# Quarter chunks in the softmax's gaps, two value chunks in one PSUM tile, and weights loaded before the last segments

## The chip, the cores and the metric

The kernel runs on one core of one Trainium2 chip. The metric is the device time of that core in microseconds (us). A kernel is timed in several executions, beside the kernel before on the same chip. In the lines of the profile PE is TensorE (PEld its weight loads), DVE is VectorE, ACT is ScalarE, POOL is GpSimd, and SPq is the DMA queue that the SP engine issues to.

## The reference, cut to what matters

Two blocks, each run twice: attention with a recurrent memory, then a gated feed-forward block.

```python
for s in range(n_seg):                      # 64 segments of 32 tokens
    h = concatenate([mem, xs])              # 8 memory rows + 32 tokens, 512 wide
    q, k, v = h @ Wq, h @ Wk, h @ Wv        # 32 heads of 128
    p = softmax(where(mask, q @ k.T * scale, -1e9))
    o = (p @ v) @ Wo
    mem = o[:8]                             # the next segment needs this
...
z = gelu(x @ w_in); z1 = z[..., :Fh]; z2 = layernorm(z[..., Fh:])
out = (z1 * (w_sp @ z2 + b_sp)) @ w_out     # Fh = 688
...
x = x + attn(ln(x)); x = x + ff(ln(x)); x = x + attn(ln(x)); x = x + ff(ln(x))
```

The 64 segments depend on one another through `mem`, so a microsecond on the path of one segment counts 128 times. The kernel reads only eight tokens of each segment later (the "last tokens" of the change); their work is cut into chunks that TensorE runs as fills while a segment waits.

## The kernel before

Three PSUM tags hold the attention's accumulators; PSUM is the memory that TensorE writes, and it is divided into banks. A tag with two buffers (`acc`) serves many tiles in turn; `attO` is one buffer of four banks.

```python
pers = ctx.enter_context(tc.tile_pool(name="a_pers", bufs=1))     # oB, VB, KTB, QTB of the last tokens
...
acc = _Tagged(ps_pool, "acc", 2)
att = _Tagged(ps_pool, "att", 1)
attO = _Tagged(ps_pool, "attO", 1)
...
# one segment, from the first scores on
scores(0)                                    # TensorE, then exp on ScalarE
qk_T(3, r3)
v0 = attO.tile([P, 4, 512], F32, name="psv0")
v_mm(0, v0[:, 0, :])                         # first value chunk, 16 matmuls
close(0)                                     # mask, VectorE
v_out(0, v0[:, 0, :])                        # cast, VectorE
scores(1)
close(1)
v1 = acc.tile([P, 512], F32, name="psv1")    # second chunk: another tile
v_mm(1, v1[:])
v_out(1, v1[:])
psM = acc.tile([P, 512], F32, name="psM")    # sums for the memory rows
...
psO = attO.tile([P, 4, 512], F32, name="psO")
pv(0)
...                                          # psD: sums for the tokens
pv(1)
...                                          # 1/x as exp(-ln x) of psM (Rm) and psD (Rt), ScalarE
...                                          # uT = psO * Rm, VectorE
spare(); fill(); fill(); run(copies)
tok_out(0)                                   # uT = psO * Rt, VectorE
pw = acc.tile([P, 512], F32, name="pw")
wo_pass(pw, uT_cur)                          # output pass, 128 matmuls
build_hA(s + 1, pw)                          # next input: copy by mask, transpose
store_o(s, pw, nc.sync)
fill(); fill(); run(copies); run(adds)
tok_out(1)
```

In the feed-forward block the first loads are `w_in` (two of 688 KB on the GpSimd queue) and three transposed loads `xnT` on the SP queue. They get the memory that `pers` gives back.

The softmax here doesn't subtract the row's maximum and nothing guards it: scores larger than these inputs give would overflow.

Of the kernel before, what the change touches and what calls it, by code (L numbers as in the profile page):

```python
# [7 lines left out]
BF16 = mybir.dt.bfloat16  # L8
# [6 lines left out]
P = 128  # L15
DM = 512
# [181 lines left out]
def b_block(tc, c, rows, xd, MV_out, RS_out, w_in, w_sp, w_out, S, first, out_final=None):  # L198
# [4 lines left out]
    with ExitStack() as ctx:  # L203
# [65 lines left out]
        def normalise(tt):  # L269
            nc.scalar.activation(out=z2n[:, tt, :], in_=z2.pop(tt)[:], func=ACT.Identity, bias=nb[tt // 2][:, tt % 2:tt % 2 + 1],  # L270
                                 scale=rs[tt // 2][:, tt % 2:tt % 2 + 1])
# [8 lines left out]
        for tt in range(NT):  # L280
            project(tt)
            if tt + 3 < NT:
                load_xnT(tt + 3)
            if tt in (9, 11, 13):
                load_wsp((tt - 9) // 2)
            if tt % 2 == 1:
                norms(tt // 2, {5: (NT - 4, NT - 3), 9: (NT - 2, NT - 1)}.get(tt, ()))
            elif tt > 1:
                normalise(tt - 2)
                normalise(tt - 1)  # L290
            if tt == 5:
                late_load(NT - 1)
        normalise(NT - 2)
# [161 lines left out]
def a_block(tc, c, rows, MV_in, RS_in, MV_out, RS_out, wqkv, Wo, S, first):  # L455
# [5 lines left out]

    with ExitStack() as ctx:

        pers = ctx.enter_context(tc.tile_pool(name="a_pers", bufs=1))
        oBr, VBr, KTBr, QTBr = {}, {}, {}, {}
        for i in range(2):
            oBr[i] = pers.tile([P, H, P], BF16, name=f"oB{i}")
            VBr[i] = pers.tile([P, 2, 4, DH], BF16, name=f"VB{i}")
            KTBr[i] = pers.tile([P, 2, 16, 32], BF16, name=f"KTB{i}")
            QTBr[i] = pers.tile([P, 2, 16, 32], BF16, name=f"QTB{i}")  # L470
        wk = ctx.enter_context(tc.tile_pool(name="a_work", bufs=2))
        blkp = ctx.enter_context(tc.tile_pool(name="a_blk", bufs=2))
        vsp = ctx.enter_context(tc.tile_pool(name="a_vs", bufs=2))
        rowp = ctx.enter_context(tc.tile_pool(name="a_rows", bufs=4))
        segp = ctx.enter_context(tc.tile_pool(name="a_seg", bufs=2))
        ps_pool = ctx.enter_context(tc.tile_pool(name="a_ps", bufs=1, space=PSUM))
        acc = _Tagged(ps_pool, "acc", 2)
        att = _Tagged(ps_pool, "att", 1)
        attO = _Tagged(ps_pool, "attO", 1)
        ctx.enter_context(tc.manual_schedule(engines=ORDERED))  # L480
# [44 lines left out]
        def run(todo):  # L525
            while todo:
                todo.pop(0)()

        def b_units(tb):
            bs = blk_state[tb]  # L530
            for j in (0, 2, 1, 3, 4, 5):
                ps = acc.tile([P, 512], F32, name="psb")
                for kts in (range(0, 2), range(2, 4)):
                    mm_chunk(ps, lambda kt, cg: bs["hB"][:, kt, :],
                             lambda kt, cg: qk_rhs(j, kt, cg) if j < 4 else v_rhs(j - 4, kt, cg), kts)
                    if kts[0] == 0:
                        yield

                def out(j=j, ps=ps):
                    if j >= 4:  # L540
                        nc.scalar.copy(bs["VB"][:, j - 4].rearrange("p i e -> p (i e)"), ps[:])
                        return
                    r = rowp.tile([P, 512], BF16, name="rowsB", bufs=2)
                    nc.scalar.copy(r[:], ps[:])
                    turns.append(lambda: nc.vector.transpose(
                        out=bs[("QTB", "KTB")[j // 2]][:, j % 2].rearrange("p a b -> p (a b)"), in_=r[:]))

                copies.append(out)
                yield
# [15 lines left out]
        def wo_last(G, heads, pwB):  # L565

            for h in heads:
                n = h // 8 * 8 + 2 * (h % 4) + h // 4 % 2
                nc.tensor.matmul(pwB[:], lhsT=oBs[G][:, n, :], rhs=Wo_sb[:, h, :].rearrange("p (kt g el) -> p g kt el", kt=4, g=4),  # L569
                                 start=(h == heads[0]), stop=(h == heads[-1]))  # L570
                if h % 2 == 1:
                    yield

        def y_part(G, q):

            pwB = acc.tile([P, DM], F32, name="pwB")
            for k, _ in enumerate(wo_last(G, range(8 * q, 8 * q + 8), pwB)):
                if k < 3:
                    yield

            def out():
                if q == 0:
                    yB[G] = wk.tile([P, DM], F32, name="yB", bufs=1)
                    nc.vector.tensor_copy(yB[G][:], pwB[:])
                else:
                    nc.vector.tensor_tensor(out=yB[G][:], in0=pwB[:], in1=yB[G][:], op=ALU.add)
                if q == 3:
                    store_last(G, nc.sync)

            adds.append(out)  # L590
            yield
# [31 lines left out]
        def segment(s, fill, spare, tail):  # L623
# [10 lines left out]
            E = segp.tile([P, 2, 4, 112], BF16, name="E")  # L634

            def qk(j):
                ps = acc.tile([P, 512], F32, name="psm")
                mm_chunk(ps, lambda kt, cg: hA_cur[:, kt, :], lambda kt, cg: qk_rhs(j, kt, cg))
                r = rowp.tile([P, 512], BF16, name="rows", tag="rowsQK", bufs=4)
                nc.scalar.copy(r[:], ps[:])  # L640
                return r
# [3 lines left out]

            def v_mm(r, ps):
                mm_chunk(ps, lambda kt, cg: hA_cur[:, kt, :], lambda kt, cg: v_rhs(r, kt, cg))

            def v_out(r, ps):
                nc.vector.tensor_copy(VA[:, r].rearrange("p i e -> p (i e)"), ps)  # L650

            def ends(q):

# [27 lines left out]
            def pv(r):  # L681

                for i in range(4):
                    for V, c0, c1 in ((VA, 0, 80), (VB, 80, 112)):
                        for g in range(2):
                            o = psO[:, 2 * r + g, 80 * i:80 * i + 80].rearrange("p (s q) -> p s q", s=2)
                            nc.tensor.matmul(o if V is VA else ends(o), lhsT=V[64 * g:64 * g + 64, r, i, :],  # L687
                                             rhs=E[64 * g:64 * g + 64, r, i, c0:c1].rearrange("p (s q) -> p s q", s=2),
                                             start=(i == 0 and V is VA), stop=True, skip_group_check=True)

            def inverse(o, in_):
                nc.scalar.activation(out=o, in_=in_, func=ACT.Ln)  # L692
                nc.scalar.activation(out=o, in_=o, func=ACT.Exp, scale=-1.0)  # L693

            def oview(b0, b1, lo, hi):
                return psO[:, b0:b1, 0:320].rearrange("p b (n q) -> p b n q", q=40)[:, :, :, lo:hi]

# [17 lines left out]
            psS = att.tile([P, 2, 512], F32, name="psS")  # L715
            scores(0)
            qk_T(3, r3)
            v0 = attO.tile([P, 4, 512], F32, name="psv0")
            v_mm(0, v0[:, 0, :])
            close(0)  # L720
            v_out(0, v0[:, 0, :])
            scores(1)
            close(1)
            v1 = acc.tile([P, 512], F32, name="psv1")
            v_mm(1, v1[:])
            v_out(1, v1[:])

            psM = acc.tile([P, 512], F32, name="psM")
            for g in range(2):
                o = psM[:, 128 * g:128 * g + 128]  # L730
                nc.tensor.matmul(o, lhsT=onesG[:, g, :], rhs=a_part(0, P, 0, 2, 0, 8), start=(g == 0), stop=True, skip_group_check=True)  # L731
# [1 line left out]
            psO = attO.tile([P, 4, 512], F32, name="psO")  # L733
            psD = att.tile([P, 2, 512], F32, name="psD")
            pv(0)
            for part, q0, q1, c0 in ((a_part, 8, 40, 0), (b_part, 8, 16, 24)):
                for r in range(2):
                    for g in range(2):
                        o = psD[:, g, 256 * r:256 * r + 256].rearrange("p (n q) -> p n q", q=32)[:, :, c0:32]
                        nc.tensor.matmul(o, lhsT=ones[64 * g:64 * g + 64, :], rhs=part(64 * g, 64 * g + 64, r, r + 1, q0, q1),  # L740
                                         start=(part is a_part and r == 0), stop=True, skip_group_check=True)
            pv(1)
            Rm = segp.tile([P, 2, 2, 64], F32, name="Rm", bufs=1)
            inverse(Rm[:].rearrange("p g r c -> p (g r c)"), psM[:, 0:256])
            Rt = segp.tile([P, 2, 512], F32, name="Rt", bufs=1)
            inverse(Rt[:], psD[:])
            for r in range(2):
                nc.vector.tensor_tensor(out=hview(uT_cur, 2 * r, 2 * r + 2, 0, 8), in0=oview(2 * r, 2 * r + 2, 0, 8),  # L748
                                        in1=Rm[:, :, r].rearrange("p g (n q) -> p g n q", q=8), op=ALU.mult)
            spare()  # L750
            fill()
            fill()
            run(copies)
            tok_out(0)
            pw = acc.tile([P, 512], F32, name="pw")
            wo_pass(pw, uT_cur)
            if s + 1 < NSEG:
                build_hA(s + 1, pw)
            if s > 0:
                store_o(s, pw, nc.sync)  # L760
            fill()
            fill()
            run(copies)
            run(adds)
# [4 lines left out]
                prep_segment(s + 1)  # L769

        ln_turn(0)
        for _ in b_units(0):
            run(turns)
            run(copies)
        run(turns)
# [3 lines left out]
        for s in range(NSEG):  # L779
# [27 lines left out]
                    rows.y_load(ys[0], first, nc.sync)  # L807

            segment(s, lambda: next(more, None), spare, tail)
        pw = acc.tile([P, 512], F32, name="pw")  # L810
        wo_pass(pw, uT[NSEG % 2])
        store_o(NSEG, pw, nc.gpsimd)
        pwB = acc.tile([P, DM], F32, name="pwB")
        for _ in wo_last(NB // 4 - 1, range(H), pwB):
            pass
        yB[NB // 4 - 1] = wk.tile([P, DM], F32, name="yB", bufs=1)
# [41 lines left out]
```

## Time and profile before

The kernel takes 1938.7 us (1938.56 to 1940.77, 3 runs).

| What | Before |
|---|---|
| span of the profiled run | 1939.8 us |
| TensorE busy | 1782.6 us, 92% |
| VectorE, ScalarE busy | 64%, 54% |
| start, to the second input transpose | 57.2 us |
| 120 segment periods (60 of each block) | 1413.8 us, 11.78 each |
| the last two periods of both blocks | 45.3 us |
| handover and tail (two feed-forward blocks with their edges) | 423.5 us |

A period is the time from one segment's input transpose (`hA<-pre`) to the next. The first period of a block is left out of the 120, since its start wanders. The handover runs from the last input transpose of the first block to the second one of the next block; the tail from the last one to the end.

Two lines of the list of waits (engine, operand, line, releaser: total us, times, longest):

```profile
DVE uT L748 <- PE psO L687: 92.2, 128, 0.8
...
DVE y_o L184 <- DMA y_o<-o_d: 7.8, 2, 4.1
```

VectorE's product uT waits for TensorE's outputs, 0.7 us a segment: it is the data's way, not the clean-up of a buffer.

### The profile page before, as it was taken

What the parts mean: (1) busy time and instruction counts of PE and PEld (TensorE: products, weight loads), DVE (VectorE), ACT (ScalarE), POOL (GpSimd) and SP (SyncE); (2) the same over time, 40 slices, a digit from 0 to 9 for tenths busy, and PEclk for the clock granted to TensorE, in tenths of its full rate; (3) what the DMA queues carried; (4) which work ended last, traced back from release to release, by engine and by line L of the source; (5) the groups of instructions that cost most, each with busy time, mean ns of one, the idle gap of its engine ahead of it and who ended that gap; (6) DMA issues with size and microseconds to landing.
All of it is one profiled execution on the core that took longest, in us unless ns stands there. A gap on an engine that the chain in (4) does not pass through costs nothing.

```text
span 1939.8 us, 94543 instructions
## 1 busy us (share of the span) xinstructions
PE 1782.6 (92%) x43776; PEld 1031.1 (53%) x43776; DVE 1247.4 (64%) x2828; ACT 1047.8 (54%) x1878; POOL 131.0 (7%) x273
## 2 busy tenths in 40 slices
PE   3999999999999999789989999999999999997898
PEld 1555555555555555435545555555555555553455
DVE  1666776787777776473346667767876777773622
ACT  1566666666666666362136666666666666663411
POOL 5000000000000000122010000000000000002000
PEclk8999999999999999989999999999999999998999
DMA  9100000021002100447730000001200120016453
GB/s 347 35 18 19 20 18 18 18 77 30 18 24 71 29 15 20 135 120 144 154 129 21 20 21 21 21 21 45 77 20 21 55 68 21 16 58 160 107 134 103
DMA packets 165524, 119.92 MB, mean 62 GB/s; under 512 B 112216, under 2 KB 140648, under 8 KB 165128
## 3 DMA queue, kind: packets, MB, share of 16 engines
q1 hardware_dynamic: 143528, 65.11, 13.4%
q0 software_dynamic: 10304, 34.07, 5.3%
q10 hardware_dynamic: 11296, 14.70, 2.6%
q8 instruction: 342, 5.60, 1.2%
q14 instruction: 54, 0.44, 0.1%
HBM read 59.29 MB, written 33.56 MB: 48 GB/s over the span
## 4 chain that ended last, share of the span: by engine, by line
PE 66%; DVE 13%; ACT 12%; issue 4%; DMA 4%; SPq 1%; POOL 0%; DVEq 0%; POOLq 0%; ACTq 0%
PE psm L503 23%; PE pw L557 10%; PE psb L503 8%; PE pg L306 7%; DVE KA L644 5%; ACT rows L640 4%; ACT E L668 4%; PE psO L687 3%; PE psS L664 3%; PE pwB L569 3%; DVE E L671 3%; PE py L331 2%; PE psM L731 2%; PE psD L740 2%; PE pz L245 1%
## 5 line engine op out<-in xcount | busy, mean ns | idle before, releaser
L503 PEld LDWEIGHTS <-hA 128*32 128x32 bf16 x12288 | 308.9, 96 | 309.1 <-DVE hA L615 47.9
L640 ACT CAST rows<-psm 128x512 bf16<-128x512 f32 x512 | 300.1, 586 | 198.0 <-PE psm L503 198.0
L557 PE MATMUL pw<-Wo_sb,uT 128*32 128x128 bf16 x16640 | 265.6, 219 | 27.0 <-issue 20.1
L503 PE MATMUL psm<-Wq_sb,hA 128*32 128x512 bf16 x4096 | 275.2, 384 | 13.3 <-DVE hA L615 12.3
L557 PEld LDWEIGHTS <-uT 128*32 128x32 bf16 x16640 | 244.5, 97 | 66.7 <-issue 28.5
L503 PE MATMUL psm<-Wk_sb,hA 128*32 128x512 bf16 x4096 | 271.0, 381 | 0.0
L503 PE MATMUL psv<-Wv_sb,hA 128*32 128x512 bf16 x4096 | 268.0, 382 | 0.0
L644 DVE STREAM_TRANSPOSE QQ<-rows 128x512 bf16<-128x512 bf16 x256 | 182.0, 711 | 86.9 <-ACT rows L640 86.6
L703 DVE TENSOR_TENSOR uT<-psO,Rt 128x384 bf16<-128x384 f32 x256 | 138.2, 540 | 125.7 <-ACT Rt L693 125.7
L644 DVE STREAM_TRANSPOSE KA<-rows 128x512 bf16<-128x512 bf16 x256 | 182.0, 711 | 39.8 <-ACT rows L640 38.4
L668 ACT ACTIVATE E<-psS 128x448 bf16<-128x448 f32 x256 | 140.0, 547 | 107.6 <-PE psS L664 107.6
L650 DVE CAST VA<-psv 128x512 bf16<-128x512 f32 x256 | 175.5, 686 | 2.4
L306 PE MATMUL pg<-z2n,wspT 128*128 128x344 bf16 x1024 | 160.1, 310 | 0.0
L664 PEld LDWEIGHTS <-KA 128*64 128x64 bf16 x2048 | 79.8, 113 | 127.8 <-DVE KA L644 126.9
L608 POOL COPY QQ<-QTB 128x256 bf16<-128x256 bf16 x128 | 51.5, 403 | 1407.6 <-PE psS L664 846.0
L693 ACT ACTIVATE Rt<-Rt 128x1024 f32<-128x1024 f32 x128 | 135.4, 1058 | 4.1
L503 PEld LDWEIGHTS <-hB 128*32 128x32 bf16 x3072 | 76.6, 97 | 101.9 <-issue 32.8
L692 ACT ACTIVATE Rt<-psD 128x1024 f32<-128x1024 f32 x128 | 128.8, 1006 | 0.0
L245 PE MATMUL pz<-w_in_sb,xnT 128*128 128x512 bf16 (+1 forms) x384 | 91.0, 401 | 36.2 <-DMA w_in_sb<-in_B_w_in_dram 17.6
L306 PEld LDWEIGHTS <-wspT 128*128 128x128 bf16 x1024 | 95.3, 98 | 52.2 <-issue 6.8
L748 DVE TENSOR_TENSOR uT<-psO,Rm 128x128 bf16<-128x128 f32 x256 | 62.5, 286 | 92.3 <-PE psO L687 92.2
L664 PE MATMUL psS<-QQ,KA 128*64 128x80 bf16 x2048 | 109.9, 208 | 10.1
(126 smaller groups left out, 2244.8 us busy)
## 6 DMA issues: line engine op xcount, KB each, us to landing
Wo_sb<-in_A_Wo_dram POOLq DMA_DIRECT2D x8, 1024.0 KB, 13.2
xs<-xd ACTq DMA_DIRECT2D x32, 256.0 KB
o_d<-o_sb SPq DMA_DIRECT2D x126, 64.0 KB
y_o<-o_d SPq DMA_DIRECT2D x24, 256.0 KB
xd<-y_o SPq DMA_DIRECT2D x22, 256.0 KB
Wq_sb<-in_A_Wq_dram POOLq DMA_DIRECT2D x8, 512.0 KB, 7.8
Wk_sb<-in_A_Wk_dram POOLq DMA_DIRECT2D x8, 512.0 KB, 11.9
Wv_sb<-in_A_Wv_dram POOLq DMA_DIRECT2D x8, 512.0 KB, 11.2
```

The lines of the kernel that those rows point to most:

```text
L245: nc.tensor.matmul(pz[:, c0:c1], lhsT=xnT[tt][:, kt, :], rhs=w_in_sb[:, kt, c0:c1], start=(kt == 0), stop=(kt == KT - 1))
L306: nc.tensor.matmul(pg[t][:, k, 0:344], lhsT=wsp[t][:, st, :], rhs=z2n[:, st, 344 * k:344 * k + 344], start=(st == 0), stop=(st == NT - 1))
L503: nc.tensor.matmul(ps[32 * cg:32 * cg + 32, :], lhsT=lhs(kt, cg), rhs=rhs(kt, cg), start=(kt == 0), stop=(kt == KT - 1), tile_position=(0, ...
L557: nc.tensor.matmul(po[32 * cg:32 * cg + 32, 0:128], lhsT=lhs[:, n, :], rhs=wo_rhs(h, cg), start=(h == 0), stop=(h == H - 1), tile_position ...
L640: nc.scalar.copy(r[:], ps[:])
L644: nc.vector.transpose(out=QQ[:, j % 2, :, 0:32] if j < 2 else KA[:, j % 2], in_=r[:])
L650: nc.vector.tensor_copy(VA[:, r].rearrange("p i e -> p (i e)"), ps)
L664: nc.tensor.matmul(pS[64 * g:64 * g + 64, i, c0:80 if K is KA else 112], lhsT=K[:, r, n:n + 2, :].rearrange("p h k -> p (h k)"), rhs=q if ...
L668: nc.scalar.activation(out=E[:, r], in_=pS, func=ACT.Exp, scale=scale)
L692: nc.scalar.activation(out=o, in_=in_, func=ACT.Ln)
L693: nc.scalar.activation(out=o, in_=o, func=ACT.Exp, scale=-1.0)
L703: nc.vector.tensor_tensor(out=hview(uT_nxt, 2 * r, 2 * r + 2, 8, 32), in0=oview(2 * r, 2 * r + 2, 8, 32), in1=Rr[:, :, :, 0:24], op=ALU.mult)
```

## The change

It means to fill TensorE's two idle gaps in the softmax, to free a buffer of `acc`, and to start the token products after half of the exp. It also moves the feed-forward block's loads forward and its norms back. The core of the diff:

```diff
-            elif tt > 1:
-                normalise(tt - 2)
-                normalise(tt - 1)
+                if tt > 1:
+                    normalise(tt - 3)
+                    normalise(tt - 2)
...
-        pers = ctx.enter_context(tc.tile_pool(name="a_pers", bufs=1))
+        olds = [ctx.enter_context(tc.tile_pool(name=f"a_old{i}", bufs=1)) for i in range(2)]
...                                          # oB, VB, KTB, QTB of i from olds[i]; pers follows
-        acc = _Tagged(ps_pool, "acc", 2)
+        accA = _Tagged(ps_pool, "accA", 1)
+        accB = _Tagged(ps_pool, "accB", 1)
...
-                for kts in (range(0, 2), range(2, 4)):
+                for kts in ((range(0, 1), range(1, 2), range(2, 4)), (range(0, 4),))[k % 2]:
...
-            v0 = attO.tile([P, 4, 512], F32, name="psv0")
-            v_mm(0, v0[:, 0, :])
+            psV = attO.tile([P, 4, 512], F32, name="psV")
+            v_mm(0, psV[:, 0, :])
+            fill()
             close(0)
-            v_out(0, v0[:, 0, :])
+            nc.vector.tensor_copy(VA[:, 0].rearrange("p i e -> p (i e)"), psV[:, 0, :])
             scores(1)
             close(1)
-            v1 = acc.tile([P, 512], F32, name="psv1")
-            v_mm(1, v1[:])
-            v_out(1, v1[:])
+            v_mm(1, psV[:, 1, :])
+            fill()
+            nc.scalar.copy(VA[:, 1].rearrange("p i e -> p (i e)"), psV[:, 1, :])
...
             pv(0)
+            pv(1)
...                                          # psD
-            pv(1)
+            fill()
...
-            inverse(Rt[:], psD[:])
+            nc.scalar.activation(out=Rt[:], in_=psD[:], func=ACT.Ln)
             for r in range(2):
...                                          # uT = psO * Rm
+                rt = Rt[:, :, 256 * r:256 * r + 256]
+                nc.scalar.activation(out=rt, in_=rt, func=ACT.Exp, scale=-1.0)
...
-            fill()
-            fill()
-            run(copies)
             tok_out(0)
...
-            fill()
             fill()
```

More of the change, by code (lines that the diff above doesn't have):

```diff
@@ L462, in a_block @@
     with ExitStack() as ctx:
-        pers = ctx.enter_context(tc.tile_pool(name="a_pers", bufs=1))
+        olds = [ctx.enter_context(tc.tile_pool(name=f"a_old{i}", bufs=1)) for i in range(2)]
         oBr, VBr, KTBr, QTBr = {}, {}, {}, {}
         for i in range(2):
-            oBr[i] = pers.tile([P, H, P], BF16, name=f"oB{i}")
-            VBr[i] = pers.tile([P, 2, 4, DH], BF16, name=f"VB{i}")
-            KTBr[i] = pers.tile([P, 2, 16, 32], BF16, name=f"KTB{i}")
-            QTBr[i] = pers.tile([P, 2, 16, 32], BF16, name=f"QTB{i}")
+            oBr[i] = olds[i].tile([P, H, P], BF16, name=f"oB{i}")
+            VBr[i] = olds[i].tile([P, 2, 4, DH], BF16, name=f"VB{i}")
+            KTBr[i] = olds[i].tile([P, 2, 16, 32], BF16, name=f"KTB{i}")
+            QTBr[i] = olds[i].tile([P, 2, 16, 32], BF16, name=f"QTB{i}")
+        pers = ctx.enter_context(tc.tile_pool(name="a_pers", bufs=1))
         wk = ctx.enter_context(tc.tile_pool(name="a_work", bufs=2))
@@ L527, in run, with b_units @@
                 todo.pop(0)()
-        def b_units(tb):
+        def b_units(tb, early=False):
             bs = blk_state[tb]
-            for j in (0, 2, 1, 3, 4, 5):
-                ps = acc.tile([P, 512], F32, name="psb")
-                for kts in (range(0, 2), range(2, 4)):
+            for k, j in enumerate((0, 2, 1, 3, 4, 5)):
+                ps = (accA if k % 2 == 0 or not early else accB).tile([P, 512], F32, name="psb")
+                for kts in ((range(0, 1), range(1, 2), range(2, 4)), (range(0, 4),))[k % 2]:
                     mm_chunk(ps, lambda kt, cg: bs["hB"][:, kt, :],
                              lambda kt, cg: qk_rhs(j, kt, cg) if j < 4 else v_rhs(j - 4, kt, cg), kts)
-                    if kts[0] == 0:
+                    if kts[-1] != KT - 1:
                         yield
@@ L570, in wo_last @@
                                  start=(h == heads[0]), stop=(h == heads[-1]))
-                if h % 2 == 1:
-                    yield
+                yield
         def y_part(G, q):
-            pwB = acc.tile([P, DM], F32, name="pwB")
+            pwB = accA.tile([P, DM], F32, name="pwB")
             for k, _ in enumerate(wo_last(G, range(8 * q, 8 * q + 8), pwB)):
-                if k < 3:
+                if k in (0, 1, 3):
                     yield
@@ L636, in qk @@
             def qk(j):
-                ps = acc.tile([P, 512], F32, name="psm")
+                ps = (accB if j < 2 else accA).tile([P, 512], F32, name="psm")
                 mm_chunk(ps, lambda kt, cg: hA_cur[:, kt, :], lambda kt, cg: qk_rhs(j, kt, cg))
@@ L647, in v_mm @@
                 mm_chunk(ps, lambda kt, cg: hA_cur[:, kt, :], lambda kt, cg: v_rhs(r, kt, cg))
-            def v_out(r, ps):
-                nc.vector.tensor_copy(VA[:, r].rearrange("p i e -> p (i e)"), ps)
             def ends(q):
@@ L689, in pv @@
                                              start=(i == 0 and V is VA), stop=True, skip_group_check=True)
-            def inverse(o, in_):
-                nc.scalar.activation(out=o, in_=in_, func=ACT.Ln)
-                nc.scalar.activation(out=o, in_=o, func=ACT.Exp, scale=-1.0)
             def oview(b0, b1, lo, hi):
@@ L717, in segment @@
             qk_T(3, r3)
-            v0 = attO.tile([P, 4, 512], F32, name="psv0")
-            v_mm(0, v0[:, 0, :])
+            psV = attO.tile([P, 4, 512], F32, name="psV")
+            v_mm(0, psV[:, 0, :])
+            fill()
             close(0)
-            v_out(0, v0[:, 0, :])
+            nc.vector.tensor_copy(VA[:, 0].rearrange("p i e -> p (i e)"), psV[:, 0, :])
             scores(1)
             close(1)
-            v1 = acc.tile([P, 512], F32, name="psv1")
-            v_mm(1, v1[:])
-            v_out(1, v1[:])
-            psM = acc.tile([P, 512], F32, name="psM")
+            v_mm(1, psV[:, 1, :])
+            fill()
+            nc.scalar.copy(VA[:, 1].rearrange("p i e -> p (i e)"), psV[:, 1, :])
+            psM = accB.tile([P, 512], F32, name="psM")
             for g in range(2):
@@ L741, in segment @@
                                          start=(part is a_part and r == 0), stop=True, skip_group_check=True)
-            pv(1)
+            fill()
             Rm = segp.tile([P, 2, 2, 64], F32, name="Rm", bufs=1)
-            inverse(Rm[:].rearrange("p g r c -> p (g r c)"), psM[:, 0:256])
+            rm = Rm[:].rearrange("p g r c -> p (g r c)")
+            nc.scalar.activation(out=rm, in_=psM[:, 0:256], func=ACT.Ln)
+            nc.scalar.activation(out=rm, in_=rm, func=ACT.Exp, scale=-1.0)
             Rt = segp.tile([P, 2, 512], F32, name="Rt", bufs=1)
-            inverse(Rt[:], psD[:])
+            nc.scalar.activation(out=Rt[:], in_=psD[:], func=ACT.Ln)
             for r in range(2):
@@ L749, in segment @@
                                         in1=Rm[:, :, r].rearrange("p g (n q) -> p g n q", q=8), op=ALU.mult)
+                rt = Rt[:, :, 256 * r:256 * r + 256]
+                nc.scalar.activation(out=rt, in_=rt, func=ACT.Exp, scale=-1.0)
+                if r == 0:
+                    run(copies)
             spare()
-            fill()
-            fill()
-            run(copies)
             tok_out(0)
-            pw = acc.tile([P, 512], F32, name="pw")
+            pw = accB.tile([P, 512], F32, name="pw")
             wo_pass(pw, uT_cur)
@@ L771, in a_block @@
         ln_turn(0)
-        for _ in b_units(0):
+        for _ in b_units(0, True):
             run(turns)
@@ L809, in a_block @@
             segment(s, lambda: next(more, None), spare, tail)
-        pw = acc.tile([P, 512], F32, name="pw")
+        pw = accB.tile([P, 512], F32, name="pw")
         wo_pass(pw, uT[NSEG % 2])
         store_o(NSEG, pw, nc.gpsimd)
-        pwB = acc.tile([P, DM], F32, name="pwB")
+        pwB = accA.tile([P, DM], F32, name="pwB")
         for _ in wo_last(NB // 4 - 1, range(H), pwB):
```

## The prediction

> **What bounds the kernel now.** I read the page's chain, then one segment of the timeline, then the timeline where an attention block (64 dependent segments, twice) hands over to the feed-forward block (twice). The chain:
>
> ```profile
> PE 66%; DVE 13%; ACT 12%; issue 4%; DMA 4%; SPq 1%; POOL 0%; DVEq 0%; POOLq 0%; ACTq 0%
> ```
>
> No engine binds alone: TensorE is 92% busy in part 1, yet a third of the chain is on other engines. One segment, cut from the timeline (start us, duration us, engine, line, operation, idle before and its releaser):
>
> ```profile
> 299.50 0.23 PE L664 MATMUL psS<-QQ,KA 128*64 128x80 bf16 x2
> 299.64 0.68 DVE L650 CAST VA<-psv 128x512 bf16<-128x512 f32 x1
> ...
> 299.87 1.05 PE L503 MATMUL psv<-Wv_sb,hA 128*32 128x512 bf16 x16
> ...
> 301.01 0.10 PEld L731 LDWEIGHTS <-onesG 128*128 128x128 bf16 x1 [0.58 <-DVE E L671]
> ...
> 301.34 0.21 PE L687 MATMUL psO<-E,VA 64*128 64x80 bf16 x2
> ...
> 301.86 0.42 ACT L693 ACTIVATE Rm<-Rm 128x256 f32<-128x256 f32 x1
> ...
> 302.18 1.01 ACT L692 ACTIVATE Rt<-psD 128x1024 f32<-128x1024 f32 x1
> ...
> 302.20 1.05 PE L503 MATMUL psb<-Wq_sb,hB 128*32 128x512 bf16 x16
> 302.38 0.49 DVE L748 TENSOR_TENSOR uT<-psO,Rm 128x128 bf16<-128x128 f32 x2 [0.71 <-PE psO L687]
> ...
> 303.07 1.96 PE L557 MATMUL pw<-Wo_sb,uT 128*32 128x128 bf16 x128
> 303.22 1.06 ACT L693 ACTIVATE Rt<-Rt 128x1024 f32<-128x1024 f32 x1
> ...
> 304.31 0.56 DVE L703 TENSOR_TENSOR uT<-psO,Rt 128x384 bf16<-128x384 f32 x1 [1.44 <-ACT Rt L693]
> ...
> 305.08 0.29 DVE L614 CAST_PREDICATED pre<-maskM,pw 128x128 bf16<-128x128 uint16 x1
> ```
>
> See three things. The second value chunk (299.87) starts while VectorE still casts the first (299.64 to 300.32), because it has another PSUM tile. The mask sum psM starts at 301.01, when VectorE's masking ends. And two paths meet at 305.08, where the next segment's input is built: TensorE's output pass (303.07 + 1.96 = 305.03) and ScalarE's log and exp of Rt, then VectorE's token products (304.31 to about 305.07). So the end of a segment is balanced to 0.05 us. Successive input transposes are 11.36 to 11.52 us apart in good segments, 11.25 without a fill, and often 0.4 to 0.8 more; over the two blocks the mean is about 11.8.
>
> The handover:
>
> ```profile
> 811.87 0.79 POOL L218 DMA_DIRECT2D w_in_sb<-in_B_w_in_dram  x1 [3.48 <-issue]
> ...
> 818.21 1.86 PE L245 MATMUL pz<-w_in_sb,xnT 128*128 128x512 bf16 x4 [6.92 <-DMA w_in_sb<-in_B_w_in_dram]
> ...
> 835.59 4.81 PE L245 MATMUL pz<-w_in_sb,xnT 128*128 128x512 bf16 x24 [1.01 <-ACT z L249]
> ```
>
> and from the list of waits (total us, times, longest):
>
> ```profile
> ACT z2n L270 <- DVE nb L265: 35.2, 15, 3.6
> ```
>
> TensorE idles about 7 us for weights that are only asked for when its last matmul ends (about 811.3), then ScalarE waits for VectorE's norms and holds the PSUM that TensorE needs.
>
> **The Trainium skill.** "PSUM — Partial Sum Buffer", section "PSUM bank collisions raise a hardware error", asks to guard PSUM by bank and quadrant; two value chunks in two banks would be safe side by side. "Perfetto Trace Analysis", section "Matmuls", wants independent groups rotated through banks so that an evacuation overlaps the next group; 299.64 against 299.87 shows just that. "TensorE: Matmul & The Clock Gate", section "What's actually happening", says that an idle TensorE falls to half clock for some 3.4 us of work: at 818 the trace's weight loads are about 0.43 us apart, later half of that, so the 7 us gap costs extra. "ScalarE: Activation LUTs", section "Rules for kernel authors", puts an activation at about 0.3 us plus 0.83 ns an element; here 256 columns take 0.417 and 1024 take 1.058, that is 0.20 + 0.835 ns an element.
>
> **The change, part by part.** I take the segment above.
>
> *First quarter, before scores(1).* A quarter is four matmuls, 0.867/4 = 0.22 us (16 chunk matmuls start 0.87 apart). The first value chunk runs 298.37 to 299.24, scores(1) waits till 299.50: it fits, delay 0 to 0.07.
>
> *Both value chunks in one tile.* This is the costly part. In the changed program's order of waits, the first matmul of the second chunk waits for VectorE's count at the cast of the first chunk: the dependency is kept per tile, though the banks differ. That cast ends at 300.32, so the chunk starts at 300.37 and not 299.87: 0.50 later. It issues until 301.24, the second quarter until 301.45, and psM starts at about 301.53: +0.52.
> The second cast, now on ScalarE, runs 301.47 to 302.06. The outputs psO reuse the chunks' banks and in the built order wait for that cast: they start at 302.11, take 0.50 (two halves of 0.24 and 0.26 today), land at 302.78. The mask path (psM to uT 1.37 us today) gives uT at 302.90.
>
> *Sums after both outputs.* psD runs 302.63 to 303.07 (0.44 as today), so Rt's log starts at 303.11 against 302.18: +0.93. The half chunk then ends at 303.40 and the output pass starts there (+0.33 against 303.07; without the smaller fill it would be +0.77).
>
> *Exp in halves.* 512 columns cost 0.20 + 0.43 = 0.63 against 1.06, so the first token product may start at 303.11 + 1.04 + 0.63 + 0.04 = 304.82: +0.51. It takes 0.76; the next input is built at 305.59 against 305.08. The output pass ends at 305.36, so VectorE's path sets the end: **+0.5 us a segment**. A segment without fill gets the same, as the cast still gates.
>
> Sum: 126 segments x 0.5 = +63. Taken off: where a residual add lies in the spare slot (16 segments with fills), the last fill now waits 0.47 us for ScalarE's cast behind the norm's log; the cast moves ahead of it, which pays back about 0.5 each: -8. About 60% of segments hold an "issue" gap of some 0.45 us; the new idle holes and the 0.2 us slack before 305.59 absorb part, a guess of -8. Attention: **+47**.
>
> *Weights early.* The split of the old pool puts w_in and the first xnT in memory whose last reader is a matmul of segment 60, and their loads now stand before the last segments. The projection can start when the final accumulator is copied, about 812.0. The second ScalarE gelu still waits for the store of yB, estimate 816.5. *Normalise one tile later* takes ScalarE's wait away: a pair of tiles costs VectorE 2.44 (statistics) + 2.65 (norms) = 5.1 us, TensorE 4.6, ScalarE 4.4, against 6.1 today (gelu at 829.98, 835.44, 841.56). Stepping through eight pairs with these, with 1.85 + 1.1 us more of VectorE in two of them, the last projection ends near 858, where today the gate matmuls start at 874.33: -16. Twice: **-32**.
>
> Net: 1938.7 + 47 - 32 = about 1953.
>
> **Rivals.** (a) The change does what its name says: TensorE's 0.43 us leave the path, the halves cut 0.4 off ScalarE, nothing new waits. For it: uT is ready at 302.67 and the output pass waits for the fill till 303.07. Then attention gains 0.05 to 0.3 a segment, and with the handover the time is 1870 to 1900. Against it: the two waits in the built order. (b) The early weights gain little, because DMA (transposes, w_sp, late rows) binds the projection: DMA is 4 to 7 tenths busy there. Then 10 instead of 32 come back, about 1975. (c) The cast is hidden: issue gaps and slack swallow half of the 0.5. Then about 1925.
>
> **Range and chances.** Attention +47 give or take 14 (the 0.5 rests on durations seen, the absorption on a guess), handover -32 give or take 6, so 1930 to 1976. Faster than 1900 needs (a): 0.04. Slower than 1977.5 needs 0.65 a segment or (b): 0.09.
>
> **What would show it.** In the profile after: a TensorE wait of about 0.5 us before the second value chunk released by VectorE's VA cast, 128 times; a wait before psO released by ScalarE's VA cast; psM 0.5 later after scores(1); input transposes 11.85 apart in good segments; psb no longer waiting 0.47 for the cast; no 7 us wait for w_in; gate matmuls starting some 46 us after the last pwB, not 63. If the chunk does not wait for VectorE, or segments stay at 11.4, I am wrong.

## More of the kernel before

`spare()` also holds the residual add of a tile of 128 finished tokens. Its operand `y_o` goes round through memory: the accumulator `yB` is stored to `o_d` on the SP queue, and `y_o` is loaded from `o_d` on the same queue.

```python
def y_add(self, tb, first, eng, store):
    o, x = self.y[tb]                                   # o: loaded from o_d
    eng.tensor_tensor(out=o, in0=o, in1=x, op=ALU.add)  # (views left out) VectorE, in its program order
```

The residual add waits little for its data (7.8 us in all). The way of that data in the timeline (start, duration, queue or engine):

```profile
767.84 0.55 SPq L563 DMA_DIRECT2D o_d<-yB  x1
...
770.63 0.33 SPq L179 DMA_DIRECT2D y_o<-o_d  x1
...
775.38 0.68 DVE L184 TENSOR_TENSOR y_o<-y_o,y_x 128x512 f32<-128x512 f32 x1
```

The load is issued 2.8 us after the store, and the add runs without a wait.

## The result, and the profile after

The changed kernel takes 1971.83 us (1970.94 to 1972.94, 4 runs), and the kernel before, with one more run, 1939.74 (1938.56 to 1945.79). The ratio is 1.0159, with a 95% interval of 1.0137 to 1.0182. A ratio is the mean time of one kernel's fast runs over that of the other's in the same rounds, so not quite the ratio of the medians. The change costs about 31 us, within 2%, where 14 were forecast.

The parts of the span:

| Part | Before | After | Change |
|---|---|---|---|
| start | 57.2 | 56.5 | -0.7 |
| 120 periods | 1413.8 | 1457.4 | +43.6 |
| last two periods of both blocks | 45.3 | 62.8 | +17.5 |
| handover and tail | 423.5 | 392.5 | -31.0 |
| span | 1939.8 | 1969.2 | +29.4 |

The chain of waits, by engine:

```profile
PE 68%; DVE 14%; ACT 9%; DMA 5%; issue 4%; POOL 1%; DVEq 0%; POOLq 0%; SPq 0%; ACTq 0%
```

TensorE is still only two thirds of it. Four lines of the list of waits:

```profile
DVE uT L748 <- ACT Rm L744: 232.4, 127, 1.9
...
PE psV L506 <- DVE VA L718: 44.4, 128, 0.4
...
DVE y_o L184 <- DMA y_o<-o_d: 16.6, 4, 7.2
ACT z2n L270 <- DVE nb L265: 16.0, 10, 2.1
```

The second line is new: TensorE waits for VectorE's cast before the second value chunk, in every segment. VectorE now stands idle 1.8 us before uT instead of 0.7; about 0.7 of that is the second cast, which it no longer makes, and so no delay. The residual add waits up to 7.2 us. The norms' wait has halved. One segment from the timeline, which answers the one in the prediction:

```profile
362.61 1.05 PE L506 MATMUL psV<-Wv_sb,hA 128*32 128x512 bf16 x16
...
363.88 0.68 DVE L718 CAST VA<-psV 128x512 bf16<-128x512 f32 x1
...
364.61 1.05 PE L506 MATMUL psV<-Wv_sb,hA 128*32 128x512 bf16 x16 [0.36 <-DVE VA L718]
...
365.70 0.59 ACT L723 CAST VA<-psV 128x512 bf16<-128x512 f32 x1 [0.87 <-PE psV L506]
...
365.81 0.23 PE L728 MATMUL psM<-E,onesG 128*128 128x128 bf16 x1
...
366.34 0.21 PE L687 MATMUL psO<-E,VA 64*128 64x80 bf16 x2
...
367.32 1.02 ACT L746 ACTIVATE Rt<-psD 128x1024 f32<-128x1024 f32 x1 [0.25 <-PE psD L738]
...
369.04 0.56 DVE L699 TENSOR_TENSOR uT<-psO,Rt 128x384 bf16<-128x384 f32 x1 [0.63 <-ACT Rt L751]
...
369.71 0.28 DVE L617 CAST_PREDICATED pre<-maskM,pw 128x128 bf16<-128x128 uint16 x1
```

Count from the first value chunk (298.37 before, as the prediction says). The second chunk starts 2.00 us after it against 1.50; psM 3.20 against 2.64; the log of psD 4.71 against 3.81; the token product 6.43 against 5.94; and the next input is built at 7.10 against 6.71.

The handover in the timeline:

```profile
784.78 0.69 DVE L589 TENSOR_TENSOR yB<-pwB,yB 128x512 f32<-128x512 f32 x1 [0.32 <-PE pwB L573]
...
785.05 3.31 SPq L231 DMA_TRANSPOSE xnT<-xb_d  x2
785.31 0.76 POOL L218 DMA_DIRECT2D w_in_sb<-in_B_w_in_dram  x1 [6.36 <-PE pwB L573]
...
788.46 0.56 SPq L567 DMA_DIRECT2D o_d<-yB  x1
...
789.08 3.06 SPq L231 DMA_TRANSPOSE xnT<-xb_d  x1
...
798.31 0.35 SPq L179 DMA_DIRECT2D y_o<-o_d  x1
800.79 0.69 DVE L184 TENSOR_TENSOR y_o<-y_o,y_x 128x512 f32<-128x512 f32 x1 [7.18 <-DMA y_o<-o_d]
...
803.66 1.90 PE L506 MATMUL psm<-Wq_sb,hA 128*32 128x512 bf16 x16 [5.99 <-DVE hA L618]
```

The w_in loads and the transposes start while almost three segments are still to come. The accumulator's store stands between the transposes on the SP queue. Its data is ready when VectorE's sum ends, at 785.47, but the store is issued only at 788.46, 3.0 us later, when two transposes have been issued; before the change it was 0.03 us later. The load of y_o is then issued 9.85 us after the store instead of 2.8. The token product stands behind the residual add in VectorE's program, so it waits too. TensorE has nothing to do for 6 us and then runs its 16 matmuls in 1.90 us instead of 1.05: the granted clock was 0.50 in 800 to 805 us. The table of stretches says what the DMA engines did (the last three columns are TensorE's clock, the DMA engines' busy share and GB/s):

```profile
785.00:790.00 5.00, 4.92 (x110) 2.38 (x103) 4.28 (x9) 2.79 (x5) 1.50 (x2) 1.00 0.95 78
790.00:795.00 5.00, 3.92 (x159) 2.91 (x153) 1.45 (x4) 3.47 (x7) 0.41 (x1) 1.00 0.91 256
795.00:800.00 5.00, 0.79 (x41) 0.61 (x41) 0.00 (x0) 0.54 (x2) 0.00 (x0) 0.88 0.75 139
800.00:805.00 5.00, 1.34 (x16) 0.54 (x20) 3.80 (x10) 0.66 (x3) 0.00 (x0) 0.50 0.29 95
```

They were nearly full for 10 us, at 95% and 91%. The Trainium skill says in "Trainium Kernel Development and Optimization", section "Key Constraints", that transfers issued from the SP, ACT and POOL queues all run on the same 16 DMA engines and interleave. The trace agrees: beside two big loads on one queue and three transposes on another, the way from a 256 KB store to its load took 9.85 us instead of 2.8. The second block shows the same, smaller: its last two periods are 29.3 us against 33.5, and 22.7 before.

And the gain, the start of the projection and of the gate matmuls:

```profile
833.26 7.08 PE L573 MATMUL pwB<-Wo_sb,oB 128*128 128x512 bf16 x32
...
841.01 9.45 PE L245 MATMUL pz<-w_in_sb,xnT 128*128 128x512 bf16 x47 [0.67 <-ACT yB L817]
...
889.50 9.50 PE L306 MATMUL pg<-z2n,wspT 128*128 128x344 bf16 x64
```

No wait for w_in stands before the projection, and from the start of pwB to the gate matmuls it takes 56.2 us instead of 70.1 (874.33 less 804.21 before).

### The profile page after: what moved, and what is told of

Same layout as the page of the kernel before. It is cut to its first block, busy times and chain, and to the rows that moved or that the text cites. A ratio compares the mean times of both kernels' runs of the same rounds, so it can differ in the third digit from the quotient of the medians.

```text
span 1969.2 us, 94605 instructions
## 1 busy us (share of the span) xinstructions
PE 1782.9 (91%) x43752; PEld 1058.7 (54%) x43776; DVE 1156.5 (59%) x2700; ACT 1139.0 (58%) x2134; POOL 131.0 (7%) x273
## 4 chain that ended last, share of the span: by engine, by line
PE 68%; DVE 14%; ACT 9%; DMA 5%; issue 4%; POOL 1%; DVEq 0%; POOLq 0%; SPq 0%; ACTq 0%
PE psm L506 23%; PE pw L561 11%; PE pg L306 7%; PE psb L506 7%; PE psV L506 7%; DVE KA L647 5%; PE psO L687 4%; DVE VA L718 4%; ACT rows L643 4%; ACT VA L723 4%; PE pwB L573 3%; PE py L331 2%; DVE E L671 2%; PE psD L738 2%; DMA Wk_sb<-in_A_Wk_dram 1%
## 5 line engine op out<-in xcount | busy, mean ns | idle before, releaser
L506 PEld LDWEIGHTS <-hA 128*32 128x32 bf16 x12288 | 321.4, 96 | 362.8 <-issue 68.8
L506 PE MATMUL psV<-Wv_sb,hA 128*32 128x512 bf16 x4096 | 268.0, 381 | 44.4 <-DVE VA L718 44.4
L506 PE MATMUL psm<-Wq_sb,hA 128*32 128x512 bf16 x4096 | 279.3, 387 | 21.3 <-DVE hA L618 18.4
L748 DVE TENSOR_TENSOR uT<-psO,Rm 128x128 bf16<-128x128 f32 x256 | 62.8, 286 | 234.9 <-ACT Rm L744 232.4
L751 ACT ACTIVATE Rt<-Rt 128x512 f32<-128x512 f32 x256 | 157.4, 629 | 4.1
L723 ACT CAST VA<-psV 128x512 bf16<-128x512 f32 x128 | 75.0, 586 | 109.3 <-PE psV L506 109.3
L671 DVE TENSOR_TENSOR E<-E,maskN 128x448 bf16<-128x448 bf16 x256 | 95.0, 371 | 41.7 <-ACT E L668 41.7
L506 PE MATMUL psb<-Wq_sb,hB 128*32 128x512 bf16 x1024 | 90.3, 389 | 26.2 <-DVE hB L521 26.2
```

The costliest lines, as they stand in the source:

```text
L506: nc.tensor.matmul(ps[32 * cg:32 * cg + 32, :], lhsT=lhs(kt, cg), rhs=rhs(kt, cg), start=(kt == 0), stop=(kt == KT - 1), tile_position=(0, ...
L671: nc.vector.tensor_tensor(out=E[:, r], in0=E[:, r], in1=maskN[:, j4, :].unsqueeze(1).to_broadcast([P, 4, 112]), op=ALU.mult)
L723: nc.scalar.copy(VA[:, 1].rearrange("p i e -> p (i e)"), psV[:, 1, :])
L751: nc.scalar.activation(out=rt, in_=rt, func=ACT.Exp, scale=-1.0)
```

## The experiments

Three batches and one more run, three rounds each, each batch beside the kernel before (median 1943.46, 1943.62, 1941.71 and 1941.76 us). All results were correct. "Periods" are the 120, "last" the last two of both blocks.

### Two tiles for the outputs instead of one (e1_split)

```diff
-        attO = _Tagged(ps_pool, "attO", 1)
+        attO = [_Tagged(ps_pool, f"attO{r}", 1) for r in range(2)]
...
-            psV = attO.tile([P, 4, 512], F32, name="psV")
+            psV = attO[0].tile([P, 2, 512], F32, name="psV")
...
-            v_mm(1, psV[:, 1, :])
+            psV1 = attO[1].tile([P, 2, 512], F32, name="psV1")
+            v_mm(1, psV1[:, 0, :])
...                                          # psO likewise in two tiles
```

> The changed kernel with the four output banks cut into two tiles of two banks; value chunk 0 and outputs 0 use the first, chunk 1 and outputs 1 the second. Theory (the per-tile wait for VectorE's first cast costs some 0.4 to 0.5 us in each of 126 segments): the wait before the second chunk goes, good segments fall from 11.73 to 11.1 to 11.4 us, time 1895 to 1925 us. Rival (the quarters, or ScalarE's extra cast, lengthen the segments): 1962 to 1982 us.

It took 1902.74 us, ratio 0.9794 (0.9777 to 0.981). Periods 1393.8 (63.6 less than after), last 59.7, handover and tail 389.5. The chain, and a segment of its timeline:

```profile
PE 84%; DMA 6%; DVE 4%; issue 3%; ACT 2%; SPq 1%; POOL 0%; DVEq 0%; POOLq 0%; ACTq 0%
```

```profile
337.74 1.05 PE L506 MATMUL psV<-Wv_sb,hA 128*32 128x512 bf16 x16
...
339.01 0.68 DVE L718 CAST VA<-psV 128x512 bf16<-128x512 f32 x1
...
339.31 1.05 PE L506 MATMUL psV<-Wv_sb,hA 128*32 128x512 bf16 x16
...
340.41 0.59 ACT L724 CAST VA<-psV 128x512 bf16<-128x512 f32 x1 [0.44 <-PE psV L506]
...
340.83 0.21 PE L687 MATMUL psO<-E,VA 64*128 64x80 bf16 x2
...
343.54 0.56 DVE L699 TENSOR_TENSOR uT<-psO,Rt 128x384 bf16<-128x384 f32 x1 [1.25 <-ACT Rt L752]
```

The chunk starts at 339.31 under the cast that runs until 339.69, and TensorE now carries 84% of the chain. But the split takes away two waits, not one. The first outputs no longer share a tile with the second chunk, so they start at 340.83 while ScalarE still casts it (until 341.00). The same holds in all 120 segments of the periods: psO starts before that cast ends, and in the changed kernel never. Counted from the first chunk, the medians fall by 0.43 us at the second chunk (2.00 to 1.57) and by 0.64 at psO (3.73 to 3.09), so about 0.2 is ScalarE's. Both waits together were worth 63.6 / 120 = 0.53 us a segment, and they were a matter of how the banks are cut into tiles. What the wait for VectorE alone costs was not measured apart.

### The same waits put into the kernel before (e4_before_psv)

```diff
-            v1 = acc.tile([P, 512], F32, name="psv1")
-            v_mm(1, v1[:])
-            v_out(1, v1[:])
+            v_mm(1, psV[:, 1, :])              # psV: the four-bank tile of the first chunk
+            nc.scalar.copy(VA[:, 1].rearrange("p i e -> p (i e)"), psV[:, 1, :])
```

> The kernel before with one part of the change alone: both value chunks in one tile of the outputs' banks, the second cast on ScalarE. Theory: 0.5 us or more a segment, as the whole fills, the log behind the cast and the whole exp stay: 1995 to 2035 us. Rival (quarters cost): 1935 to 1955 us.

It took 2033.66 us, ratio 1.0461 (1.0446 to 1.0477). Periods 1501.1, that is 87.3 more than before, or 0.73 each. The shared tile alone, with its second cast on ScalarE, costs more than the whole change does, so other parts of the change pay back.

### The fills as before (e2_fills, e8_split_fills)

```diff
-                for kts in ((range(0, 1), range(1, 2), range(2, 4)), (range(0, 4),))[k % 2]:
+                for kts in (range(0, 2), range(2, 4)):
...                                          # no fill after the value chunks; two after psD, two at the end
```

> The changed kernel with the last-token chunks put back as halves in their old places. Theory: the wait of 0.4 to 0.5 us stays and a whole chunk stands before the output pass again, so 1975 to 2000 us. Rival (the quarters in the two gaps are what costs): 1935 to 1955 us.

> The split outputs' tile (no TensorE wait for the first cast), with the fills of before: halves, none in the two new gaps, two after the sums and two at the end. Tells what the quarters are worth without the wait. Theory: the gaps of the softmax are idle TensorE time whatever the tile, two quarters a segment are 0.43 us of TensorE that move there, and the run without them in the changed kernel lost 35 us; so 1925 to 1942 against 1902.7 with the quarters. Rival (the quarters gain only in the hole that the wait makes): 1896 to 1910.

In the changed kernel: 2007.0 us, ratio 1.0325 (1.0308 to 1.0342), periods +34.0. In the split kernel: 1919.44, ratio 0.9887 (0.9858 to 0.9917), periods +14.0. So the quarters, with their new places, help in both. They are worth more in the changed kernel; that the wait makes a hole for them there is my reading, not shown apart. I had the first too low and the second too high.

### The exp whole again (e11_split_whole_exp)

```diff
             nc.scalar.activation(out=Rt[:], in_=psD[:], func=ACT.Ln)
+            nc.scalar.activation(out=Rt[:], in_=Rt[:], func=ACT.Exp, scale=-1.0)
...
-                rt = Rt[:, :, 256 * r:256 * r + 256]
-                nc.scalar.activation(out=rt, in_=rt, func=ACT.Exp, scale=-1.0)
```

> The split outputs' tile with the exp of Rt whole again. In the split kernel's segment VectorE's first token product waits for the first half of the exp and ends 0.25 to 0.3 us before TensorE's output pass; the whole exp would start it 0.45 later, so about 0.2 us later than TensorE's end. Theory: +0.2 us in each of 120 segments and more, 1918 to 1932 against 1902.7. Rival (TensorE's pass sets the end anyway and the halves are worth nothing): 1898 to 1910.

It took 1920.8 us, ratio 0.9897 (0.9874 to 0.9919); periods 1411.4, 17.6 more than the split kernel. The halves are worth 0.15 us a segment, as a slack of 0.25 to 0.3 us before the end of TensorE's pass let one expect.

### The loads late again (e3_late_loads)

```diff
-        olds = [ctx.enter_context(tc.tile_pool(name=f"a_old{i}", bufs=1)) for i in range(2)]
+        pers = ctx.enter_context(tc.tile_pool(name="a_pers", bufs=1))
+        olds = [pers, pers]
```

> The changed kernel with the old single pool, so w_in and the first three transposes load only after the last accumulator. Theory (the early loads hold up the residual rows and so the last two segments of each block, 17.5 us in all, against some 20 us that they save at the handover): the last two periods of a block add up to under 26 us instead of 33.5 and 29.3, the gap from the last projection weights to the first projection is 6 to 8 us again, time 1966 to 1980 us. Rival (the long last segments have another cause): those periods stay above 28 us and the time rises above 1985 us.

It took 1980.05 us, ratio 1.0187 (1.0172 to 1.0203). Last 47.3 (15.5 less than after), handover and tail 410.0 (17.5 more), with the old wait back:

```profile
842.32 0.58 PE L245 MATMUL pz<-w_in_sb,xnT 128*128 128x512 bf16 x1 [6.99 <-DMA w_in_sb<-in_B_w_in_dram]
```

So the early loads gain 17.5 us at the handover and lose 15.5 in the last segments.

### The norms in the old order (e7_norm_back)

```diff
-                if tt > 1:
-                    normalise(tt - 3)
-                    normalise(tt - 2)
+            elif tt > 1:
+                normalise(tt - 2)
+                normalise(tt - 1)
```

> The changed kernel with the feed-forward's normalisation in the order of before. With all loads late the handover and the tail together took 394.7 us against 410.0 before and 377.4 after, so by subtraction the order of the norms is worth 15 us and the early loads 17. Theory: 15 come back, time 1982 to 1992, ScalarE's wait for the norms back above 30 us in all. Rival (the projection is held by DMA anyway and the early loads gave all): 1971 to 1977.

It took 1980.88 us, ratio 1.0196 (1.0181 to 1.0211), a little below the range. Handover and tail 402.7, 10.2 more than after, and ScalarE waits again:

```profile
ACT z2n L270 <- DVE nb L265: 37.6, 15, 3.6
```

### Which of the early loads does the harm (e5_gate, e9_late_xnT, e10_late_win)

A tile that segment 62 still reads (`KA0`) is put into the memory that the loads take over, so that they wait for it. First for the whole of it:

```diff
+            if i == 0:
+                KA0 = olds[0].tile([P, 2, 16, 32], BF16, name="KA0")
             oBr[i] = olds[i].tile([P, H, P], BF16, name=f"oB{i}")
...
-        KAr = [pers.tile([P, 2, 16, 32], BF16, name=f"KA{i}") for i in range(2)]
+        KAr = [KA0, pers.tile([P, 2, 16, 32], BF16, name="KA1")]
```

> The changed kernel, but one small tile that is read until segment 62 lies in front of the freed memory, so that the two loads of w_in (688 KB each) start about 1.5 segments later; the transposed rows xnT stay early. Theory (the early w_in loads crowd out the accumulator's way through memory, the residual add waits, VectorE holds up the next segment): the last two periods of the blocks, 33.5 and 29.3 us after the change, fall to 24 to 28 each, and the handover stays near 191; time 1953 to 1964. Rival A (the transposes on the same queue as the accumulator's store do it): the last two periods stay above 30 in block 1, time 1967 to 1974. Rival B (the later loads no longer land in time): the periods fall, but the handover is 3 to 8 us longer each time, 1964 to 1976, as in the run with all loads late.

It took 1965.66 us, ratio 1.0116 (1.0099 to 1.0133). Last 47.2: the excess is gone. But handover and tail were 401.9, 9.4 more, as rival B said. The text was wrong in one thing: the transposes had moved too (issued at 806.86), so rival A was not tested.

So the freed memory was cut into two pools, one exactly as large as w_in, and KA0 was put into one or the other:

```diff
+        # pool "A" lies under w_in, pool "B" under xnT
+        # e9:  A = oB0, VB0, pad       B = KA0, KTB0, QTB0
+        # e10: A = KA0, oB0, pad       B = VB0, KTB0, QTB0
```

> In the gate run both w_in and the three transposed loads of xnT turned out to start late, so it did not tell them apart, though its text said so. Here only the xnT transposes wait for segment 62, w_in starts early as in the changed kernel. The last two periods of the two blocks together are 62.8 us after the change and 47.2 with the gate. Theory W (the 1.4 MB of w_in crowd out the accumulator's way through memory): they stay above 56, time 1968 to 1976. Rival X (the transposes stand in the SP queue before the accumulator's store): they fall to 47 to 50, time 1960 to 1968.

> The mirror image: only w_in waits for segment 62, the xnT transposes start early (even a segment earlier than in the changed kernel). Theory W: the last two periods fall to 47 to 50 in all, time 1960 to 1968. Rival X: they stay above 56, time 1968 to 1976. If both this run and the other stay high, each is enough alone; if both fall, it takes the two together.

With late transposes: 1964.93 us, ratio 1.0122 (1.0098 to 1.0146), last 49.8, handover and tail 394.5. With late w_in: 1962.38, ratio 1.0102 (1.0082 to 1.0123), last 47.3, handover and tail 395.7. The lines for the accumulator's way, first with late transposes, then with late w_in:

```profile
790.07 0.69 DVE L597 TENSOR_TENSOR yB<-pwB,yB 128x512 f32<-128x512 f32 x1 [0.32 <-PE pwB L581]
...
790.79 0.55 SPq L575 DMA_DIRECT2D o_d<-yB  x1
...
796.32 0.33 SPq L179 DMA_DIRECT2D y_o<-o_d  x1
```

```profile
774.18 5.00 SPq L231 DMA_TRANSPOSE xnT<-xb_d  x3
...
790.42 0.56 SPq L575 DMA_DIRECT2D o_d<-yB  x1
...
793.21 0.35 SPq L179 DMA_DIRECT2D y_o<-o_d  x1
```

From store to load it is 5.5 us beside w_in, 2.8 without it, and 9.85 in the changed kernel, beside both. Theory W falls: w_in alone costs 49.8 - 47.2 = 2.6 us of the 15.6. What the transposes alone cost is not shown. In e10 they did not stay where the changed kernel has them: they ran a segment earlier, and the last was issued by 779.18, 11 us before the store, so the two never met. So the case named last in the expectation of e10, that it takes the two together, is not shown either.

The traces do show that the transposes take part, in the changed kernel, as rival X said: there the store is issued 3.0 us after its data is ready (2.2 in the second block), behind two transposes on its queue, and in e9, where none stand there, 0.03 us after. The two w_in loads also landed in 9.7 us (median of the two, first block) beside the transposes and in 6.2 without. A run with w_in late and the transposes in their place would tell the two from the pair; it was not made.

### Both findings together (e6_split_gate, e12_best)

> The split outputs' tile and the later w_in together. If the two costs are separate they add: 1902.7 less the gain of the gate alone, 1886 to 1897 by the theory, 1897 to 1906 by rival A or B. The best candidate so far.

> The split outputs' tile with w_in alone late, as in the run that did only that to the changed kernel, where the handovers and the tail took 452 us against 458 with the gate. If the two findings stay separate: the last two periods 45 in all, the time 1884 to 1891, against 1890.8 with split and gate. Rival (the handover is held by something that neither touches): 1891 to 1897.

Split and gate: 1890.78 us, ratio 0.9735 (0.9714 to 0.9756). Split and late w_in alone: 1889.77, ratio 0.9736 (0.9704 to 0.9768), periods 1391.2, last 45.0, handover and tail 393.5. The two kernels can't be told apart. Both add up as expected (the 452 and 458 us of that expectation count the start in, 56.7 and 56.5), and both beat the kernel before by 2.6%.

## Why the prediction was right or wrong

The range held, but the size was off: +31 instead of +14, in the direction that the prediction named.

- **Both value chunks in one tile: right.** The steps of one segment came out at +0.50 (second chunk), +0.56 (psM), +0.90 (log of psD), +0.49 (token product), for +0.50, +0.52, +0.93 and +0.51; the next input came at +0.39, for +0.51. Both waits are there: the list puts psO's wait down to ScalarE's cast only 14 times, but in all 120 segments psO starts after that cast, 0.05 us after its end in the segment shown. That taking both waits away gave back 63.6 us, where the sum said 63, is partly luck. The 63 was for the whole segment against the kernel before, with the later sums and the halved exp in it; the 63.6 is for the waits alone, inside the changed kernel.
- **The sum for attention: right, how it comes about less so.** +43.6 for 120 periods, and some 2 of the +17.5, make about 46 for +47. Of the two -8 one was called a guess. For the other, TensorE's waits for ScalarE's rowsB cast before psb fell from 18 to one, and from 11.7 us to 3.8, as it said. What pays back is measured otherwise: with both waits gone the rest of the change gains 20.0 us of periods (1413.8 to 1393.8), of it 14.0 by the quarters and 17.6 by the halves of the exp, if they add. Then something else costs about 12, and which part was not tried.
- **Weights early: this is the step that failed.** It said that "their loads now stand before the last segments" and counted only the gain. Putting them back showed both sides: they gain 17.5 us and cost 15.5 in the last two segments of the blocks. The way is shown step by step in the trace: the store behind the transposes, the late load of y_o, the residual add that waits 7.2 us, the token product behind it, and TensorE idle for 6 us. Moving the transposes later, or w_in later and the transposes earlier, takes nearly all of it away. The missing term, 15.5, is the difference between 14 and the 29.4 of the two profiled spans.
- **Norms a tile later: right in kind.** 10.2 us for the order alone. The 6.1 us a pair that the prediction took for the kernel before is the longer of its two gaps; from 829.98 to 835.44 it is 5.5. With the 17.5 of the loads that is 27.7 of the 31.0, against the forecast 32. The gate matmuls start 49 us after the last pwB ends (840.34 to 889.50), where 46 were forecast and 63 stood before.
- **The rivals.** (a) was realised by the split tile: 1902.7 us, just above its 1870 to 1900, and 1889.8 with w_in late as well. What speaks for it, uT ready at 302.67, is read off the first of two products; the second ends at 302.87. Its condition, no wait, failed in the changed kernel. (b) named DMA and 1975 us, close to the result, but for another reason: the projection gained as expected, and DMA struck the attention instead. (c) did not happen.

What stays open: how the 15.5 us divide between the transposes and the pair with w_in. The gate run's handover is 6 to 7 us longer than that of the two halves of it. The 120 periods of the five kernels with the same segment (after, e3, e5, e9, e10) lie between 1457.4 and 1462.0, so differences of about 4 us there mean nothing. And in the slow segment TensorE also stood 2.0 us for which the profile names no wait ("issue", in front of 796.88); that full DMA engines delayed its instructions is only argued.

## What to carry to other kernels

In these kernels a dependency is kept per tile: two banks in one tile waited for one another's readers (second chunk at 2.00 us), and two tiles in two banks did not (1.57), so cut tiles along what is read and written at the same time. When a load is moved forward, list what small transfers go round through memory in that stretch, what will stand before them on their own queue, and which engine's program has work behind them. An expected gain at one edge should be entered with its cost at the other.

## What the Trainium skill lacked or had wrong

- "PSUM — Partial Sum Buffer", section "PSUM bank collisions raise a hardware error": guarding by bank would allow the two chunks side by side, and the runs agree (1902.7 us with two tiles). It lacks that a kernel's waits can be coarser than the bank: one tile over several banks cost 0.35 us of TensorE's waiting for VectorE on average (44.4 us in 128 segments), and with the wait for ScalarE 0.53 us of path a segment.
- "Trainium Kernel Development and Optimization", section "Key Constraints": that the queues share the DMA engines is right. It gives no size for what big loads do to a small round trip: 2.8 us alone, 5.5 beside 1.4 MB, 9.85 beside that and three transposed loads, and 3.0 us before it for two transposes ahead of it on its own queue.
- "TensorE: Matmul & The Clock Gate", section "What's actually happening": half clock after idling is right (1.90 us for 1.05, granted clock 0.50). The page's budget is about 3.4 us of work; here it lasted about 5 (three groups of 16, 803.66 to 808.76). The page also says that its window is free-running and the number varies, so this is a size and no contradiction.
- "ScalarE: Activation LUTs": nothing is wrong, but the prediction quoted the rule for a bias pointer (0.3 us). For immediate scale and bias the section "What ACT_TABLE_LOAD costs" gives 186 ns and 0.833 ns an element, and the trace agrees: 0.20 and 0.835, and 0.63 us for the half exp of 512 columns.
